# Warm-up products in bf16 in place of fp32, and first touches of the inputs moved close together

## The chip, the cores and the metric

The kernel runs on one core of a Trainium2 chip. The metric is the device time of one execution in microseconds. A core has a matrix engine (TensorE, PE in the profile; its weight loads are listed as PEld), a vector engine (DVE), a scalar engine (ACT), GpSimd (POOL) and a queue processor (SP). DMAs are issued by SP and, for a few, by ACT. The engines run side by side and wait for each other by semaphores.

## The reference

Linear attention over eight batches is followed by a feed-forward layer with exact GELU:

```python
q_s = exp(q - max(q, -1));  q_s = q_s / sum(q_s, -1)       # (8, 8, 576, 64), over the head dimension
k_s = exp(k - max(k, 2));   k_s = k_s / sum(k_s, 2)        # over the sequence
kv  = einsum('bhsd,bhse->bhde', k_s, v)
x   = einsum('bhsd,bhde->bhse', q_s, kv)                   # reshaped to (4608, 512)
h   = x @ w_in                                             # (512, 2048)
out = (0.5 * h * (1 + erf(h / sqrt(2)))) @ w_out           # (2048, 512)
```

The inputs are float32 and so is the output.

## The kernel before

The work is cut by batch. Of each batch the first 512 of the 576 sequence rows make one block of 512 tokens; the remaining 64 rows of all eight batches make a ninth block. A block goes through these steps, all products in bf16: `exp_q` and `exp_k` on ACT, `norm_q` (row sums, reciprocals and the product with them, on DVE and POOL), a transpose of the normalised q, `cast_v` (v to bf16 with a column of ones), `kv_mm` and `kv_norm` (k times v and the division by the column of sums), `x_mm` (q times kv), then `h_phase` (16 groups of four products with w_in into PSUM, each followed by a GELU on ACT) and `y_phase` (four groups of 16 products with w_out, copied by DVE and stored).

The order on each engine is the order in which the code issues the instructions (`manual_schedule`). The steps of the next batches are issued inside the loops of the current one, as functions that `h_phase` and `y_phase` call at given places.

Batch 0 has nothing before it to hide behind, and it is where the change lies. The order there is: ACT issues four small DMAs into the tile `touch` (line 423), SP issues the loads of q, k, v of batch 0, then w_in in five pieces (`load_wi`, line 363), three pieces of w_out, q and k of batch 1, and so on. DVE clears `zeros32` and `zeros` (lines 436 and 437). PE then multiplies zeros by zeros (`warm`, line 405), transposes the first half of q (line 212), multiplies zeros twice more, transposes the second half, multiplies zeros twice more, and goes on to `kv_mm` (line 166), four products of zeros in `warm_x` (line 413), `x_mm` (line 251) and the first `h_phase` (line 295). POOL normalises the first half of q (line 198), casts three quarters of v (line 145) and then the first two pieces of w_in (line 375); DVE casts the other pieces (line 379).

DMAs issued by SP and ACT share eight completion semaphores, given out in turn, so that a ninth DMA is not issued before the first has landed, and so on. The four touches take four of them.

Of the kernel before, what the change touches and what calls it, by code (L numbers as in the profile page):

```python
# [8 lines left out]
FP32 = mybir.dt.float32  # L9
# [7 lines left out]
def kernel(  # L17
# [16 lines left out]
    nc = tc.nc  # L34
# [9 lines left out]
    NS = S // 64  # L44
    VW = D + 2

    singles = ctx.enter_context(tc.tile_pool(name="singles", bufs=1))
# [19 lines left out]

    kvc = [singles.tile([128, HP, D], BF16, name=f"kvc{b}") for b in range(B)]
    zeros = singles.tile([128, 512], BF16)
    zeros32 = singles.tile([128, 512], FP32)  # L70
    scr = singles.tile([128, 2], FP32)

    def setup_tiles():
        nc.vector.memset(scr, 0.0)
        for i in range(2):
            nc.vector.memset(v_aug[i][:, :, :, D:D + 1], 1.0)
# [23 lines left out]
    def load(b):  # L100
        load_main(b, "q", q)
        load_pair(b, "k", k)
        load_pair(b, "v", v)
# [295 lines left out]
            out=wo_bf[:, 4 * i + c0:4 * i + c0 + n, :], in_=w[:, c0:c0 + n]  # L399
        )  # L400

    def warm(n, z=zeros):
        ps = psum_y.tile([128, DM], FP32, tag="y")
        for i in range(n):
            nc.tensor.matmul(ps, z[:, 0:128], z, start=True, stop=True)  # L405

    def warm_x():

# [6 lines left out]
                )  # L415

    touch = singles.tile([16, 4, 2], FP32)
    for i, a in enumerate((k[0].rearrange("h (p n) d -> (h p) (n d)", n=NS)[0:128:8, 0:2],  # L420
                           v[0].rearrange("h (p n) d -> (h p) (n d)", n=NS)[0:128:8, 0:2],
                           moe_w_in[0:128:8, 0:2], moe_w_out[0:512:32, 0:2])):
        nc.scalar.dma_start(out=touch[:, i, :], in_=a)


# [7 lines left out]
    wo.append(load_wo(3, 2))  # L433
    load_pair(1, "v", v, 4)
    load(2)
    nc.vector.memset(zeros32, 0.0)  # L436
    nc.vector.memset(zeros, 0.0)
    setup_tiles()
    warm(5, zeros32)


    table(AF.Exp)
# [5 lines left out]
    tp_evac(0, 0, "s")  # L448
    table(AF.Gelu)
    warm(2)  # L450
    cast_v(0, 0)
    for hp in range(1, HP):
        cast_v(0, hp, nc.gpsimd)
    cast_wi(0, wi[0], "p")
    cast_wi(1, wi[1], "p")
    tp_mm(0, 1)
    warm(2)
    for hp, pool, tag in ((0, psum_y, "y"), (1, psum_y, "y"), (2, psum_a, "a"), (3, psum_h, "h")):
        x_tile(0, hp, pool, tag)
# [151 lines left out]
```

## Time and profile before

| | us |
|---|---|
| median of 4 executions | 283.81 (283.62 to 283.97) |
| the profiled execution | 283.77 |
| its span, first to last instruction | 282.0 |
| PE busy | 269.8 |
| ACT busy | 156.8 |
| DVE busy | 102.1 |
| POOL busy | 32.9 |
| products of zeros at line 405, 14 records, sum | 8.1 |
| start of the first w_in product (line 295) | 14.76 |

A record in the timeline gives its start, its length, the engine, the line, the tiles with their sizes, a count, and in brackets how long the engine sat idle before it and what released it. PE records overlap, since products are pipelined: a product of 512 columns is recorded as 379 ns long while such products follow each other every 217 ns. A line of a table of stretches gives the stretch, its length, the busy time and count of each engine, the granted clock, the busy share of the DMA engines and their rate in GB/s.

### The profile page before, as it was taken

The numbers are of one execution on the slowest core, as the hardware profiler recorded it, in microseconds if no ns is written. First come the engines' busy times: TensorE is split into PE (matmuls) and PEld (weight loads), VectorE is DVE, ScalarE is ACT, GpSimd is POOL, SyncE is SP. The second block draws the span as 40 slices with busy tenths as digits, with TensorE's granted clock in tenths as the row PEclk, the third lists the DMA queues.
The fourth block names the chain that finished last, engine by engine and source line by source line (L and its number), as shares of the span: only waits on it lengthen the run. The fifth ranks groups of instructions, "written<-read, shape, count | busy, mean of one in ns | idle before, by whom it ended". The sixth has DMA issues, their size and how long they took to land.

```text
span 282.0 us, 4527 instructions
## 1 busy us (share of the span) xinstructions
PE 269.8 (96%) x1894; PEld 125.8 (45%) x1922; DVE 102.1 (36%) x150; ACT 156.8 (56%) x242; POOL 32.9 (12%) x25
## 2 busy tenths in 40 slices
PE   7799999999999899999999999999999999999993
PEld 3344454444444344444444444444444444444442
DVE  3766576309750560084007500651016100220011
ACT  5766654689377815692469346843683363136300
POOL 0530050002020050005000500050005000000000
PEclk9999999999999999999999999999999999999999
DMA  7999999953349339801991199117401500120033
GB/s 244 390 400 428 400 400 406 402 210 85 107 111 364 121 115 256 341 37 45 240 372 55 40 215 380 45 70 187 113 0 74 149 2 0 74 77 0 0 77 76
DMA packets 44852, 50.10 MB, mean 178 GB/s; under 512 B 20384, under 2 KB 29856, under 8 KB 44576
## 3 DMA queue, kind: packets, MB, share of 16 engines
q1 hardware_dynamic: 44544, 49.68, 51.6%
q8 instruction: 15, 0.25, 0.3%
q10 hardware_dynamic: 288, 0.13, 0.2%
q14 instruction: 5, 0.04, 0.0%
HBM read 36.70 MB, written 9.44 MB: 164 GB/s over the span
## 4 chain that ended last, share of the span: by engine, by line
PE 66%; DMA 23%; DVE 3%; ACT 3%; SPq 1%; issue 1%; ACTq 0%
PE ps L305 33%; PE ps L295 29%; DMA f<-in_v_dram 8%; DMA w<-in_moe_w_in_dram 6%; DMA f<-in_k_dram 5%; DMA out_dram<-y_sb 3%; DMA touch<-in_moe_w_out_dram 2%; PE kv L166 1%; PE ps L327 1%; DVE v_aug L145 1%; PE ps L251 1%; ACT ek L138 1%; DVE qsum L196 1%; ACT e L133 1%; DVE e L198 1%
## 5 line engine op out<-in xcount | busy, mean ns | idle before, releaser
L295 PE MATMUL ps<-xT,wi_bf 128*128 128x512 bf16 x565 | 125.4, 379 | 0.6
L305 PE MATMUL ps<-wo_bf,g 128*128 128x512 bf16 x543 | 122.3, 379 | 2.8 <-DVE y_sb L312 1.2
L300 ACT ACTIVATE g<-ps 128x512 bf16<-128x512 f32 x144 | 85.6, 597 | 67.3 <-PE ps L295 67.3
L295 PEld LDWEIGHTS <-wi_bf 128*128 128x128 bf16 x576 | 56.0, 98 | 68.4 <-issue 0.5
L305 PEld LDWEIGHTS <-g 128*128 128x128 bf16 x560 | 54.0, 98 | 65.6 <-issue 1.9
L312 DVE COPY y_sb<-ps 128x512 f32<-128x512 f32 x35 | 23.8, 683 | 75.2 <-PE ps L305 72.1
L198 POOL TENSOR_TENSOR e<-e,recq 128x2048 bf16<-128x2048 bf16 (+1 forms) x9 | 25.7, 2857 | 178.0 <-DVE recq L197 145.9
L145 DVE CAST v_aug<-f 128x576 bf16<-128x576 f32 x26 | 17.9, 745 | 57.3 <-DMA f<-in_v_dram 57.3
L277 ACT CAST xT<-ps 128x512 bf16<-128x512 f32 x19 | 10.2, 588 | 31.8 <-PE ps L251 22.2
L196 DVE TENSOR_REDUCE qsum<-e 128x16 f32<-128x1024 bf16 (+1 forms) x13 | 21.0, 1616 | 14.5 <-ACT e L133 14.5
L133 ACT ACTIVATE e<-f 128x512 bf16<-128x512 f32 (+1 forms) x42 | 20.5, 556 | 2.2 <-DMA f<-in_q_dram 2.0
L138 ACT ACTIVATE ek<-f 128x2304 bf16<-128x2304 f32 (+1 forms) x10 | 17.2, 1730 | 1.9 <-DMA f<-in_k_dram 1.8
L275 DVE CAST xT<-ps 128x512 bf16<-128x512 f32 x15 | 9.7, 686 | 15.4 <-PE ps L251 12.6
L79 ACT ACT_TABLE_LOAD x9 | 11.5, 1283 | 2.8 <-issue 2.6
L405 PE MATMUL ps<-zeros 128*128 128x512 f32 (+1 forms) x14 | 8.1, 722 | 1.5 <-DVE zeros L436 1.5
L133 ACT ACT_TABLE_LOAD x7 | 9.0, 1283 | 0.1
L166 PEld LDWEIGHTS <-ek 64*64 64x64 bf16 x576 | 6.6, 105 | 3.3 <-issue 1.6
L379 DVE CAST wi_bf<-w 128x512 bf16<-128x512 f32 (+1 forms) x8 | 7.1, 916 | 2.0 <-DMA w<-in_moe_w_in_dram 1.8
L166 PE MATMUL kv<-v_aug,ek 64*64 64x65 bf16 x576 | 7.4, 193 | 0.4 <-POOL v_aug L145 0.2
L398 DVE CAST wo_bf<-w 128x2048 bf16<-128x2048 f32 (+1 forms) x5 | 5.1, 1014 | 4.8 <-DMA w<-in_moe_w_out_dram 4.8
L198 DVE TENSOR_TENSOR e<-e,recq 128x1024 bf16<-128x1024 bf16 x4 | 6.4, 1600 | 0.1
L251 PE MATMUL ps<-qT,kvc 64*64 64x512 bf16 x60 | 5.0, 390 | 1.4 <-DVE kvc L177 1.4
(33 smaller groups left out, 41.5 us busy)
## 6 DMA issues: line engine op xcount, KB each, us to landing
out_dram<-y_sb SPq DMA_DIRECT2D x32, 256.0 KB, 2.3
f<-in_k_dram SPq DMA_DIRECT2D x6, 1152.0 KB, 9.7
f<-in_v_dram SPq DMA_DIRECT2D x6, 1152.0 KB, 11.5
f<-in_q_dram SPq DMA_DIRECT2D x6, 1024.0 KB, 7.3
w<-in_moe_w_in_dram SPq DMA_DIRECT2D x6, 512.0 KB, 8.1
f<-in_k_dram SPq DMA_DIRECT2D x4, 576.0 KB, 10.1
f<-in_v_dram SPq DMA_DIRECT2D x8, 288.0 KB, 8.2
f<-in_q_dram SPq DMA_DIRECT2D x4, 512.0 KB, 8.5
```

The lines of the kernel that those rows point to most:

```text
L79: nc.scalar.activation(out=scr[:, 1:2], in_=scr[:, 0:1], func=func)
L133: nc.scalar.activation(out=dst[:, i], in_=src[:, u], func=AF.Exp)
L138: nc.scalar.activation(out=ek[b % 2][:, i:i + n], in_=st[b]["kf"][:, i:i + n].rearrange("p x (n d) -> p x n d", n=NS), func=AF.Exp,)
L145: eng.tensor_copy(out=v_aug[b % 2][:, hp, :, 0:D], in_=st[b]["vf"][:, hp, :].rearrange("p (n d) -> p n d", n=NS),)
L166: nc.tensor.matmul(ps[c, i, half, 0:D + 1], ek[b % 2][pr, hp, n, :], v_aug[b % 2][pr, hp, n, 0:D + 1], start=(n == 0), stop=(n == NS - 1),)
L196: nc.vector.reduce_sum(out=qsum, in_=eq[:, :, hs, :], axis=AX.X)
L198: eng.tensor_tensor(out=eq[:, :, hs, :], in0=eq[:, :, hs, :], in1=recq.unsqueeze(3).to_broadcast([128, J, w, D]), op=ALU.mult,)
L277: nc.scalar.copy(out=st[b]["xT"][:, hp, :], in_=ps)
L295: nc.tensor.matmul(ps, wi_bf[:, dm, t * 128:(t + 1) * 128], xT[:, dm, :], start=(dm == 0), stop=(dm == NDM - 1),)
L300: nc.scalar.activation(out=g[:, t, :], in_=ps, func=AF.Gelu)
L305: nc.tensor.matmul(ps, st[c]["g"][:, t, j * 128:(j + 1) * 128], wo_bf[:, t, :], start=(t == 0), stop=(t == NDF - 1),)
L312: nc.vector.tensor_copy(out=y_sb, in_=ps)
```

## The change

The warm-up ahead of the first transposes is 25 products of bf16 zeros in place of five of fp32 zeros; the fp32 tile and its memset are gone. The four touches still read 16 times 8 bytes each, but from other rows. Of k and v they read the first 16 sequence rows of the first head, which lie in 4 KB, in place of 16 rows of 2304 bytes spread over the first 128 such rows. Of w_in they read rows 0 to 15 in place of every eighth of the first 128 rows; of w_out rows 0 to 15 in place of every 32nd of the first 512.

The order of every other instruction on every engine, and the waits of SP, ACT and POOL, are the same.

```diff
-    zeros32 = singles.tile([128, 512], FP32)
...
-    def warm(n, z=zeros):
+    def warm(n):
         ps = psum_y.tile([128, DM], FP32, tag="y")
         for i in range(n):
-            nc.tensor.matmul(ps, z[:, 0:128], z, start=True, stop=True)
+            nc.tensor.matmul(ps, zeros[:, 0:128], zeros, start=True, stop=True)
...
     touch = singles.tile([16, 4, 2], FP32)
-    for i, a in enumerate((k[0].rearrange("h (p n) d -> (h p) (n d)", n=NS)[0:128:8, 0:2],
-                           v[0].rearrange("h (p n) d -> (h p) (n d)", n=NS)[0:128:8, 0:2],
-                           moe_w_in[0:128:8, 0:2], moe_w_out[0:512:32, 0:2])):
+    for i, a in enumerate((k[0, 0, 0:16, 0:2], v[0, 0, 0:16, 0:2],
+                           moe_w_in[0:16, 0:2], moe_w_out[0:16, 0:2])):
         nc.scalar.dma_start(out=touch[:, i, :], in_=a)
...
-    nc.vector.memset(zeros32, 0.0)
     nc.vector.memset(zeros, 0.0)
     setup_tiles()
-    warm(5, zeros32)
+    warm(25)
```

## The prediction

> **What bounds the kernel now.** I read the page's busy times first, then what TensorE (PE) waits for, then the first 23 us in order of time, and last the DMA rate in short stretches.
>
> ```profile
> PE 269.8 (96%) x1894; PEld 125.8 (45%) x1922; DVE 102.1 (36%) x150; ACT 156.8 (56%) x242; POOL 32.9 (12%) x25
> ```
>
> PE is busy for 269.8 of 282.0 us. Whatever waits it has are few, and they are listed:
>
> ```profile
> PE ps L405 <- DVE zeros L436: 1.5, 1, 1.5
> PE ps L251 <- DVE kvc L177: 1.4, 3, 0.6
> PE ps L305 <- DVE y_sb L312: 1.2, 1, 1.2
> PE ps L212 <- POOL e L198: 1.0, 1, 1.0
> PE kv L166 <- POOL v_aug L145: 0.2, 1, 0.2
> ```
>
> Four of the five lie wholly or mostly before 14.8 us, where batch 0 is prepared; the exception is the 1.2 us at 98 us. From 14.76 us (the first product with w_in) on, PE does not wait before the kv step at 41.7 us for more than a few hundredths. So the end is set by **when that first product starts**, and by the pace of the loads while PE is just in time with them. What leads up to it:
>
> ```profile
> 9.33 0.62 PE L212 MATMUL ps<-identity,e 128*128 128x128 bf16 x8 [0.97 <-POOL e L198]
> 11.14 2.15 POOL L145 CAST v_aug<-f 128x576 bf16<-128x576 f32 x3 [1.87 <-DMA f<-in_v_dram]
> 11.86 0.47 PE L166 MATMUL kv<-v_aug,ek 64*64 64x65 bf16 x34 [0.17 <-POOL v_aug L145]
> 13.96 2.58 POOL L375 CAST wi_bf<-w 128x512 bf16<-128x512 f32 x4 [0.67 <-DMA w<-in_moe_w_in_dram]
> 14.41 0.41 PE L251 MATMUL ps<-qT,kvc 64*64 64x512 bf16 x4 [0.59 <-DVE kvc L177]
> 14.75 7.02 PEld L295 LDWEIGHTS <-wi_bf 128*128 128x128 bf16 x34 [0.23 <-POOL wi_bf L375]
> 22.14 6.16 PEld L295 LDWEIGHTS <-wi_bf 128*128 128x128 bf16 x30 [0.37 <-DVE wi_bf L379]
> ```
>
> (Start, length, engine, line, tiles, count, and in brackets the idle time and its releaser.) The v casts start when a load of v lands, the kv step waits for them, the w_in cast starts when w_in lands at 13.96, and at 22.14 the weights for w_in's fourth piece come just in time from its cast. All of it is the same load stream: q, k, v, w_in in this order. A stream later by d moves PE's whole remainder by about d. The warm-up product, by contrast, is over before 9.33, when PE waits for POOL's normalised q.
>
> The stream's rate (stretch, busy times, DMA share, GB/s at the end):
>
> ```profile
> 2.00:2.50 0.50, 0.50 (x2) 0.03 (x1) 0.01 (x1) 0.00 (x0) 0.00 (x0) 1.00 0.59 115
> 2.50:3.00 0.50, 0.50 (x2) 0.31 (x1) 0.00 (x0) 0.38 (x1) 0.00 (x0) 1.00 0.91 311
> 5.00:6.50 1.50, 1.50 (x4) 0.69 (x3) 0.79 (x1) 1.36 (x5) 0.00 (x0) 1.00 1.02 348
> 6.50:8.00 1.50, 1.50 (x5) 0.55 (x3) 1.47 (x3) 0.56 (x2) 0.63 (x1) 1.00 1.02 386
> 11.00:12.50 1.50, 1.33 (x44) 0.54 (x41) 0.28 (x2) 1.48 (x2) 1.30 (x2) 1.00 1.06 387
> ```
>
> Summing rate times length, 0.99 MB have moved by 5.0 us, 2.09 by 8.0 and 3.26 by 11.0. q is 1.05 MB, k and v 1.18 each: k begins at about 5.2 us, v at 8.4, w_in at 11.4. The stream runs near 390 GB/s once started.
>
> **The change part by part.** The sum is made against the profiled execution: 283.77 us, of which 282.0 are span and 1.8 lie around it. The median is 283.81, so the same number serves.
>
> *The fp32 memset goes.* It is 0.48 us of DVE, 0.91 to 1.39. The bf16 memset (0.27 us) takes its place and ends at 1.18; PE started 0.06 after its memset, so it starts at 1.24 in place of 1.45. DVE is next wanted at 5.71, after 3.70 us idle, and ACT's table load at 2.62 follows its own DMA issues. Gain on the path: 0.
>
> *Five fp32 products become 25 bf16 ones.* The weight loads tell the pace of the fp32 ones, and when the clock opens:
>
> ```profile
> 5.03 0.34 PEld L405 LDWEIGHTS ps<-zeros 128*128 128x128 f32 x1 [0.52 <-issue]
> 5.88 0.34 PEld L405 LDWEIGHTS ps<-zeros 128*128 128x128 f32 x1 [0.52 <-issue]
> 6.48 0.19 PEld L405 LDWEIGHTS ps<-zeros 128*128 128x128 f32 x1 [0.26 <-issue]
> 6.91 0.19 PEld L405 LDWEIGHTS ps<-zeros 128*128 128x128 f32 x1 [0.24 <-issue]
> ```
>
> Ten records: 0.85 us apart up to 5.88, then 0.43, so the speed doubles near 6.0, some 4.6 us after PE's start. A bf16 product of 512 columns takes 0.217 us warm (13.87 us for 64 of them after 14.76), half a warm fp32 record; slow, I take half of 0.85, 0.427. If the doubling again comes 4.6 us after the start, at 5.84, then 4.60 / 0.427 = 10.8 products are slow, 14.2 x 0.217 = 3.1 us follow, and the warm-up ends at 8.9. Before it ends at 8.36. The transposes cannot start before 9.27, when POOL ends its product: the 0.5 us later is hidden, with 0.4 to spare. Past that, PE sits 0.4 us idle before the kv step at 11.47, so about 0.75 us in all before lateness shows, one for one. The 45 more PE instructions stand ahead of the transposes only. Cost taken 0, by the row that shows the opening. Bounds: 0, and 2.25 if it never opened before the transposes (25 x 0.427 = 10.7 us, so the end is at 11.9, less the cover up to 9.67).
>
> A rule to weigh: the Trainium skill, "TensorE: Matmul & The Clock Gate", Part 1, says that the gate opens after a busy window of about 3.4 us which runs free of the program. An estimate by that rule alone puts the opening 3.4 to 6.8 us after the start, the end of the 25 between 8.3 and 10.0, and the cost between 0 and 0.35 us, where the row gives 0. The rule speaks against this change, since 25 products outlast the 20 half-records of before in every phase of such a window.
>
> *The rest of PE's order* (two warm products behind each transpose group, four between kv and x) is the same in both, so the gap of 0.97 us before 9.33 only shrinks. 0.
>
> *The four touches move.* ACT still issues four DMAs of 16 times 8 bytes (0.44 us each). k and v are now read within 4 KB, w_in within 16 rows and w_out within 16 rows, where they were spread over 8 times or more of that. Two costs can follow.
>
> First, landing:
>
> ```profile
> touch<-in_k_dram ACTq DMA_DIRECT2D x1, 0.1 KB, 2.2
> touch<-in_moe_w_out_dram ACTq DMA_DIRECT2D x1, 0.1 KB, 5.3
> ```
>
> SP's issues wait for touches, since eight completion semaphores are shared in turn: the first part of w_in is issued at 7.46, just as the w_out touch lands. SP waits 1.1 us there. But at 7.46 3.41 MB were issued and only 1.89 moved: 1.5 MB, or 3.9 us, still stand ahead of it. Sooner landing gains nothing, up to some 2 us later costs nothing. 0.
>
> Second, the first bytes of each tensor. q is touched by nothing, and its start is slow: until 3.0 only 0.23 MB moved against 1.5 us x 390 = 0.59, a loss of 0.9 us, part of which must be plain start-up. k, touched, shows 348 in place of 390 for 1.5 us: a loss of 0.16. v and w_in show none. If the rows near a touch are what saves this, moving them away brings a loss back for k, v and w_in. Against it: the rows of w_in from 128 on, and most of k and v, are touched in neither kernel and stream at 386 to 393. Bounds: 0.16 gained (k's dip goes, nothing comes), and 2.6 lost (three tensors at 0.9, less k's 0.16). I take the row nearest, k's dip, for v and w_in as well: 2 x 0.16 = 0.3.
>
> Sum: 0 + 0 + 0 + 0.3 = **0.3 us, 284.1**, which is within 0.2% (0.57 us, about what a measurement of this kernel can tell from no change).
>
> **The rivals.**
> *A, the touches matter more* (slower): k, v and w_in each start as slowly as half of q's start, 3 x 0.45 less 0.16 = 1.2, so 285.0. For it: q's slow start, and that the old touches lay at every eighth of the first 128 rows that the loads read, the new ones at one end. Against: no dip at untouched rows. It decides, that is passes 0.57, once each start loses 0.25.
> *B, the warm-up runs long* (slower): the clock opens late and the 25 push the transposes, the kv step and the first w_in product, by up to the 2.25 worked above, half of it as the middle case: 284.9. It decides when more than 0.75 + 0.57 us are added to the end at 8.9, which takes six more slow products, an opening 2.7 us later than the trace's. Against: at the trace's pace 14 of the 25 come after the opening.
> *C, faster*: touches that fall close together return sooner and leave the engines to q in its start, while they land now at 2.2 to 5.3 us beside it. If half of the 0.9 us comes back and k's dip goes, 0.45 + 0.16 = 0.6 is gained, 283.2, since q, k, v and w_in all move up. It decides at two thirds of q's loss. Against: 64 reads of 8 bytes are nothing beside 1 MB.
> *D, nothing at all*: only hidden things move, 283.8.
>
> **How the numbers follow.** Forecast with D (283.5 to 284.4): 0.41. A: 0.31. B: 0.09. C: 0.19. So faster 0.19, same 0.41, slower 0.40. The range reaches from C with a little more (283.0) to past A (285.3, that is 1.5 lost); the upper bounds of A and B are left out. The forecast's own range is 283.3 to 284.4.
>
> **What would show it.** Right: 25 warm-up products ending near 8.9, transposes still released by POOL's product near 9.3, w_in's first cast near 14.0 to 14.3 and the first w_in product as much later; the rate at 8 to 9.5 and 11 to 12.5 us dipping by some 10%. A: rates under 300 there, and the w_in cast after 14.9. B: bf16 products still 0.43 apart after 8 us, the transposes after 9.6. C: the stream past 300 GB/s before 2.5 us. I am wrong if PE waits later than 14.8 us change by more than the start did.

## The result, and the profile after

The changed kernel takes 283.10 us (median of 39 executions, 282.44 to 283.64) where the kernel before takes 283.81 (59 executions): a ratio of 0.9974, 95% interval 0.9968 to 0.9981, so 0.7 us faster. The forecast was 0.3 us slower. The profiled execution of the changed kernel took 283.21 us with a span of 281.4, against 283.77 and 282.0.

The front of the kernel, on which the prediction was spent, went nearly as it said. The timeline of the changed kernel (line numbers are lower by one from the tiles on, by three at the touches and by four behind the memset of the zeros):

```profile
1.19 7.90 PE L404 MATMUL ps<-zeros 128*128 128x512 bf16 x25 [1.19 <-DVE scr L73]
5.43 0.15 PEld L404 LDWEIGHTS <-zeros 128*128 128x128 bf16 x1 [0.28 <-issue]
5.86 2.73 PEld L404 LDWEIGHTS <-zeros 128*128 128x128 bf16 x13 [0.27 <-issue]
9.40 0.62 PE L211 MATMUL ps<-identity,e 128*128 128x128 bf16 x8 [0.32 <-POOL e L197]
13.92 2.56 POOL L374 CAST wi_bf<-w 128x512 bf16<-128x512 f32 x4 [0.63 <-DMA w<-in_moe_w_in_dram]
14.75 3.78 PEld L294 LDWEIGHTS <-wi_bf 128*128 128x128 bf16 x19 [0.23 <-POOL wi_bf L374]
19.70 9.39 PEld L294 LDWEIGHTS <-wi_bf 128*128 128x128 bf16 x45 [1.17 <-DVE wi_bf L378]
```

The 25 products run from 1.19 to 9.09, their weight loads 0.43 us apart up to 5.86 and half that after it. The transposes still wait for POOL. The first w_in product starts at 14.76 in both kernels. The one difference is a wait of 0.68 us on PE for w_in's third piece, at 19.70; most of it is made good at the kv step of batch 1, where the kernel before waited 0.4 us.

In the profiled executions, one of each kernel, PE's last product ends at 277.55 us before and at 277.66 after: 0.1 us **later**. Yet the span is 0.5 us shorter. So everything that this pair gains, and 0.1 more, lies behind PE's last product, in the last 4 us, which the prediction did not look at. The DMA issues of the kernel before in the last 5 us (tiles, queue, count, size, us from issue to landing), and what SP waits for there (us in total, times, the longest):

```profile
out_dram<-y_sb SPq DMA_DIRECT2D x1, 96.0 KB, 2.2
out_dram<-y_sb ACTq DMA_DIRECT2D x1, 96.0 KB, 2.8
out_dram<-y_sb SPq DMA_DIRECT2D x1, 32.0 KB, 2.9
out_dram<-y_sb ACTq DMA_DIRECT2D x1, 32.0 KB, 3.1
```

```profile
SPq L606 <- DMA out_dram<-y_sb: 2.5, 2, 1.7
```

The same of the changed kernel:

```profile
out_dram<-y_sb SPq DMA_DIRECT2D x1, 32.0 KB, 2.0
out_dram<-y_sb ACTq DMA_DIRECT2D x1, 32.0 KB, 2.1
```

```profile
SPq L602 <- DMA out_dram<-y_sb: 1.6, 2, 1.3
```

The last two stores, the same in both programs, land 0.9 and 1.0 us sooner. What else the DMA engines carried then stands in the DMA queues between 279 and 281 us (packets, MB, share of the time of 16 DMA engines). Of the kernel before:

```profile
q10 hardware_dynamic: 135, 0.09, 17.3%
q1 hardware_dynamic: 82, 0.03, 6.1%
q14 instruction: 1, 0.01, 1.0%
```

Of the changed kernel:

```profile
q10 hardware_dynamic: 157, 0.13, 21.4%
q1 hardware_dynamic: 96, 0.04, 7.1%
```

In the kernel before, one packet of queue 14, an instruction fetch, stands among the last stores; in the changed kernel it does not. The packet records behind these views tell more:

```
kernel before   instruction packet, 8192 bytes, starts 279.47, 0.31 us
                last five store packets of 512 bytes: 279.85 to 280.19, 68 to 85 ns each (from 279.42 to 279.82: 25 to 40)
                last store: 15 of its 16 parts landed by 280.12, the last part at 281.00
changed kernel  instruction packet, 8192 bytes, starts 281.74, after the last instruction
                no store packet of 512 bytes over 60 ns after 279.4
                last store: 15 of 16 parts landed by 280.15, the last part at 280.18
```

A store is done when its last part is. Of each of the last two stores one part of 16 came 0.9 us after the other fifteen (the other store's at 280.82, its fifteenth at 279.91). The records do not name the DMA engine; the reading is that one engine fetched instructions while its parts of the last stores stood in its queue. How a fetch of 0.31 us makes 0.9 is not shown: the late packets end 0.6 us after the others, and 0.3 us more than for the others passes from there to the landing.

Whose instructions? The change takes one instruction from DVE, a memset, and adds 45 to PE by the prediction's count (the trace has 30 records more, half of them weight loads). In the trace, DVE's own steps point to itself: two of its steps in the barrier at the program's end, where the engines wait for each other, 0.12 us apart in the kernel before, are 0.48 apart in the changed one (280.62 and 281.10), and the same gap appears 128 recorded instructions earlier, at 68.19. 8192 bytes are 128 instructions of 64 bytes, if 64 is taken as the size. An earlier fetch of queue 14 also moves, from 65.83 to 69.38 us; the other three of the span stay near 40, 106 and 170. So the theory to test, **T**: DVE's last instruction fetch falls where DVE's instruction count puts it; one instruction fewer moves it from among the last stores to behind them. The rivals are **F1**, the touches, and **F2**, the bf16 warm-up. All three can be separated by kernels that change one and keep the rest. A further rival is the place in memory: without the fp32 tile, by the code, every tile behind it lies 2048 bytes lower in each partition.

### The profile page after: what moved, and what is told of

Read it like the earlier page. It is cut to its first block, busy times and chain, and to the rows that moved or that the text cites. A ratio compares the mean times of both kernels' runs of the same rounds, so it can differ in the third digit from the quotient of the medians.

```text
span 281.4 us, 4556 instructions
## 1 busy us (share of the span) xinstructions
PE 270.7 (96%) x1909; PEld 126.0 (45%) x1937; DVE 101.8 (36%) x149; ACT 156.8 (56%) x242; POOL 32.9 (12%) x25
## 4 chain that ended last, share of the span: by engine, by line
PE 81%; DMA 10%; DVE 3%; ACT 2%; issue 1%; SPq 1%; ACTq 0%
PE ps L304 38%; PE ps L294 38%; DMA f<-in_v_dram 6%; DMA w<-in_moe_w_in_dram 3%; PE kv L165 2%; DMA f<-in_q_dram 1%; PE ps L250 1%; PE ps L326 1%; DVE v_aug L144 1%; DVE qsum L195 1%; ACT ek L137 1%; ACT e L132 1%; DVE e L197 1%; SPq L230 0%; DVE y_sb L311 0%
## 5 line engine op out<-in xcount | busy, mean ns | idle before, releaser
L404 PE MATMUL ps<-zeros 128*128 128x512 bf16 x29 | 9.1, 476 | 1.2 <-DVE scr L73 1.2
```

## The experiments

Times are medians; ratios are to the kernel before on the same chip, with 95% intervals. "Tail" is the span's end less the end of PE's last product, in the profiled execution. What was found in all of them:

| run | DVE instructions against before | last fetch, us after PE's end | tail, us | time, us | ratio |
|---|---|---|---|---|---|
| kernel before | 0 | 1.9 | 4.41 | 283.81 | |
| changed kernel | -1 | 4.1 | 3.77 | 283.10 | 0.9974 (0.9968 to 0.9981) |
| touch_only | 0 | 1.9 | 4.42 | 283.75 | 0.9997 (0.9979 to 1.0016) |
| warm_bf16_same_count | 0 | 1.9 | 4.53 | 283.94 | 1.0000 (0.9988 to 1.0011) |
| fp32_one_memset | -1 | 4.1 | 3.76 | 282.81 | 0.9957 (0.9940 to 0.9974) |
| after_one_more | 0, and a new tile | 2.0 | 4.45 | 287.37 | 1.0110 (1.0075 to 1.0145) |
| after_scr_twice | 0 | 1.9 | 4.43 | 283.97 | 0.9997 (0.9985 to 1.0009) |
| after_pad8 | -1, and a new tile | 4.1 | 3.77 | 286.65 | 1.0102 (1.0077 to 1.0127) |
| after_five_more | +4 | -2.3 | 3.44 | 282.55 | 0.9957 (0.9942 to 0.9971) |
| after_three_fewer | -4 | 4.6 | 3.45 | 283.04 | 0.9972 (0.9952 to 0.9992) |
| before_four_more | +4 | -2.2 | 3.44 | 282.57 | 0.9953 (0.9933 to 0.9973) |
| before_four_more_touch | +4 | -2.0 | 3.46 | 282.99 | 0.9974 (0.9959 to 0.9988) |
| after_five_more_again | +4 | -2.3 | 3.46 | 282.97 | 0.9972 (0.9957 to 0.9986) |

**The touches alone**, in the kernel before:

```diff
-    ... k[0].rearrange("h (p n) d -> (h p) (n d)", n=NS)[0:128:8, 0:2], ...
+    ... k[0, 0, 0:16, 0:2], v[0, 0, 0:16, 0:2], moe_w_in[0:16, 0:2], moe_w_out[0:16, 0:2] ...
```

> The kernel before with the four new touches and nothing else. Theory T (the gain is in the tail: one DVE instruction fewer moves DVE's last 8 KB instruction fetch from 279.5 us, amid the last stores, to after them): DVE's instructions are those of before, so the fetch stays and the time is that of before, 283.8 within 0.2, with the last store landing some 3 us after its issue. Rival F1 (the touches give the gain): 283.1.

No gain: 0.9997, and a tail of 4.4 us. F1 falls.

**The warm-up alone**, with the now unread fp32 tile still cleared:

```diff
-    warm(5, zeros32)
+    warm(25)
```

> The kernel before with the 25 bf16 warm-up products, but the fp32 memset kept, so that DVE has as many instructions as before. Theory T: 283.8 within 0.2, and the fetch among the last stores. Rival F2 (the warm-up in bf16 gives the gain, by 45 more PE instructions or by a warmer clock): 283.1.

1.0000, tail 4.5. F2 falls: neither the 45 PE instructions nor the other clock history in the first 9 us is worth anything.

**One DVE instruction fewer**, with the old warm-up and touches:

```diff
-    zeros = singles.tile([128, 512], BF16)
     zeros32 = singles.tile([128, 512], FP32)
+    zeros = zeros32[:, 0:256].bitcast(BF16)
...
-    nc.vector.memset(zeros, 0.0)
```

> The kernel before, fp32 warm-up and old touches kept, with one DVE instruction fewer: the bf16 zeros are the first half of the cleared fp32 tile, and their own memset goes. Theory T: 283.1 within 0.2, the last DVE fetch after the last stores, which land 2.0 to 2.4 us after their issue. Rivals F1 and F2: 283.8.

The whole gain is there, 0.9957 (the interval overlaps with the changed kernel's), and the fetch and tail are those of the changed kernel. In this kernel the warm-up and the touches, which the change was about, are the old ones. Its SP wait and landings at the end:

```profile
SPq L605 <- DMA out_dram<-y_sb: 1.5, 2, 1.3
```

```profile
out_dram<-y_sb SPq DMA_DIRECT2D x1, 32.0 KB, 2.0
out_dram<-y_sb ACTq DMA_DIRECT2D x1, 32.0 KB, 2.1
```

**One DVE instruction more in the changed kernel**, first with a tile of its own:

```diff
     zeros = singles.tile([128, 512], BF16)
+    extra = singles.tile([128, 2], FP32)
...
     nc.vector.memset(zeros, 0.0)
+    nc.vector.memset(extra, 0.0)
```

> The changed kernel with one more DVE instruction, a memset of 8 bytes a partition behind that of the zeros, where DVE is idle. Theory T: the fetch is back among the last stores and the time back at 283.8 within 0.2. Rivals F1 and F2: 283.1, since touches and warm-up are those of the changed kernel.

The tail went back to 4.4 us, as T says, but the time went to 287.37: 3.5 us too much, and all of it ahead of PE's end, which came at 281.78. This run changed two things at once, an instruction and an address: the new tile moves every tile behind it by 8 bytes. Two runs take these apart, one with the instruction and no tile, one with the tile and no instruction:

```diff
         nc.vector.memset(scr, 0.0)
+        nc.vector.memset(scr, 0.0)
```

> The changed kernel with the 8-byte memset of the tile scr issued twice: as many DVE instructions as the kernel before, and no tile more, so that no address moves. Theory T (the place of DVE's last instruction fetch): 283.8, the span's end 4.4 us after PE's end as in the kernel before. Rival A (the 4 us that the run with a new 8-byte tile lost come from the instruction itself): 287.

```diff
+    pad = singles.tile([128, 2], FP32)
     scr = singles.tile([128, 2], FP32)
```

> The changed kernel with an unused tile of 8 bytes a partition ahead of scr and no instruction more. Theory B (the run with the new tile lost its other 3.5 us because every later tile, the targets of the loads among them, moved by 8 bytes): 286.6, the loads' rate between 30 and 50 us near 380 GB/s in place of 402, and the end still 3.8 us after PE's end. Rival A: 283.1.

The instruction gives 0.9997 and a tail of 4.4: the changed kernel with its gain undone by one memset of 8 bytes that DVE issues in an idle time at 1 us. That is T's clearest run, and since all tiles lie there as in the changed kernel, the place in memory falls as a rival too. Its landings and SP's wait at the end are again those of the kernel before:

```profile
out_dram<-y_sb SPq DMA_DIRECT2D x1, 32.0 KB, 2.9
out_dram<-y_sb ACTq DMA_DIRECT2D x1, 32.0 KB, 3.1
SPq L603 <- DMA out_dram<-y_sb: 2.5, 2, 1.7
```

The tile gives 286.65 with a tail of 3.8, as theory B has it: the moved addresses cost the time, and not the instruction. The loads' rate is the last number of each stretch; of the changed kernel:

```profile
15.00:30.00 15.00, 14.22 (x65) 6.34 (x66) 10.05 (x11) 9.70 (x17) 1.38 (x3) 1.00 1.04 411
30.00:50.00 20.00, 19.82 (x174) 9.39 (x175) 13.16 (x21) 11.35 (x19) 3.90 (x4) 1.00 1.05 402
```

Of the run with the unused 8 bytes:

```profile
15.00:30.00 15.00, 14.73 (x64) 6.46 (x63) 9.28 (x11) 8.92 (x16) 1.90 (x4) 0.89 1.04 401
30.00:50.00 20.00, 19.16 (x170) 9.13 (x172) 13.95 (x21) 10.48 (x17) 3.90 (x4) 1.00 1.06 380
```

The DMA engines are as busy and carry 2.4 and 5.5% less. In the packet records, the mean packet of 2304 bytes up to 60 us takes 99.4 ns in place of 94.9, one of 1024 bytes 50.1 in place of 46.9, while DVE's copies of y take 683 ns in place of 684. The loads are slower; DVE is not. The Trainium skill, "DMA: Bandwidth & Descriptors", section on how a descriptor splits into AXI transactions, describes extra beats for a descriptor that starts off a 256-byte boundary, and speaks of bytes that are fetched; here the source in DRAM did not move, only the target in SBUF, and no run here shows the beats. So why the packets take 3 to 5 ns more is open. In the pad run the granted clock also falls to a half from 15.0 to 18.4 us (the 0.89 above), and in the run with the tile `extra` from 101.9 to 105.4; in no other profile here does it fall before PE's end. That is the smaller part of the loss: of the pad run's six executions two had a mean granted clock of 1.000 and still took 286.35 and 285.59 us, 2.5 to 3.3 more than the changed kernel; the four at 0.993 and 0.994 took 286.33 to 287.90, on average 1.1 more than those two.

**Moving the fetch further away**, to earlier and to later:

```diff
-        nc.vector.memset(scr, 0.0)
+        for i in range(6):
+            nc.vector.memset(scr, 0.0)
```

> The changed kernel with the memset of scr issued six times: four DVE instructions more than the kernel before. Theory T: the last fetch is asked for some four instructions earlier, behind the copy at 274 us, and is over before the last stores are issued; DVE has no stall at its last barrier either (0.48 us between its last two barrier steps in the changed kernel, 0.12 before). The end 3.4 us after PE's, 282.7. Rival C (any number of DVE instructions above the changed kernel's loses): 283.8.

```diff
-        nc.vector.memset(scr, 0.0)
+        nc.gpsimd.memset(scr, 0.0)
         for i in range(2):
-            nc.vector.memset(v_aug[i][:, :, :, D:D + 1], 1.0)
+            nc.gpsimd.memset(v_aug[i][:, :, :, D:D + 1], 1.0)
```

> The changed kernel with three of its DVE memsets (scr and the two of v_aug) issued on POOL, which is idle there. Theory T: DVE's stream ends at or ahead of the place that asks for the last fetch, so there is no fetch and no stall: the end 3.4 us after PE's, 282.7. Rival C': fewer instructions bring nothing beyond the first one, 283.1.

Both have the tail of 3.4 us that was expected, 0.3 less than the changed kernel, and DVE's stall at the last barrier is gone too (0.11 us between the two steps). With five memsets more, the fetch starts at 275.64, ahead of the last stores. With three fewer it still takes place, at 281.97, after the last instruction; that there would be none was wrong. The times, 282.55 and 283.04, have intervals that overlap with each other's and with that of the changed kernel, so the last 0.3 us is shown in the profiles and not in the times; by its time alone, 283.04, rival C' would fit as well.

**Are touches or warm-up worth anything besides?** With the fetch out of the way in all three, on one chip. The first two are the kernel before, without and with the new touches, and with this edit; the third is the changed kernel with five memsets more, again:

```diff
-        nc.vector.memset(scr, 0.0)
+        for i in range(5):
+            nc.vector.memset(scr, 0.0)
```

> The kernel before, fp32 warm-up and old touches, with the memset of scr issued five times, so that DVE's instruction count is that of the fastest kernel so far (the changed one with five memsets more). Theory T: the end 3.4 us after PE's, about 1.0 us less than the kernel before, 282.8. Rivals F1 and F2 (touches or warm-up are worth something besides): 283.1 or more, since both are those of the kernel before.

> The same with the new touches as well: fp32 warm-up, DVE's count as in the run beside it. Theory T: the same time as that run, within 0.2. The prediction's term (the first rows of v and w_in stream 0.3 us later under the new touches): 0.3 more.

> The changed kernel with the memset of scr issued six times, again, on the chip of the two runs beside it: bf16 warm-up and new touches, the same DVE count. Theory T: the same time as those two within 0.2, with PE's end alike and 3.4 us behind it.

The kernel before, with four memsets added, is at 282.57: its ratio is below the changed kernel's (0.9953 against 0.9974), but the intervals overlap. The two runs with the new touches are 0.4 us above it, where T expected 0.2 at most. The means of 7 and 12 executions (282.59 and 282.96, standard deviation 0.45) differ by 0.37 with an interval of about 0.45 to either side, and the run touch_only showed nothing of the kind. So a cost of the new touches of some tenths is neither shown nor excluded. The bf16 warm-up costs nothing that can be seen: 282.99 and 282.97.

## Why the prediction was wrong

*The step that failed* is the first term of the sum, put at nothing: "The fp32 memset goes ... Gain on the path: 0." DVE is idle where the memset stood, and as work it costs nothing; that was right. But it is also an instruction, and DVE's instruction count sets where in time its last fetch falls. Taking it away brought the last store's landing from 3.45 us after PE's end (281.00 less 277.55) to 2.52 (280.18 less 277.66), a gain of 0.93; of that the new stall at the last barrier gave back 0.3, by the time from the landing to the end of the span (281.95 less 281.00 is 0.95, 281.43 less 280.18 is 1.25). The tail became 0.63 shorter, where the medians differ by 0.71.

*The frame that let it happen*: the prediction said that the end is set by when the first w_in product starts, and costed only what lies ahead of it. The profile of before had the lines against that. Its last two stores of 32 KB landed 2.9 and 3.1 us after their issue, while the larger ones of 96 KB just ahead took 2.2 and 2.8, and the page counts five instruction packets in queue 14:

```profile
q14 instruction: 5, 0.04, 0.0%
```

No rival covered the tail. The faster one, C, named 283.2, which is near the measured 283.10, but by luck: its gain was to lie in the start of the stream, which was to pass 300 GB/s before 2.5 us. From 2.0 to 2.5 us it ran at 150 GB/s (115 before), and PE's first w_in product starts at 14.76 in both. C's threshold was off as well: with k's dip counted, as in its 0.6, a gain of 0.57 needs under half of q's 0.9 and not two thirds.

*The warm-up term* was right in its cost of 0: 25 products ending at 9.09 where 8.9 was predicted, an opening of the clock near 5.9, where 5.84 was, and transposes released by POOL with 0.32 us to spare; the run with it alone is at 1.0000. That the opening came so near the predicted place was in part luck: over all thirteen profiles the granted clock opens between 2.8 and 5.9 us after PE's first product, not at a fixed 4.6. The rule on a window that runs free, which the prediction weighed, has such a spread, 3.4 to 6.8 in its estimate; the 2.8 of fp32_one_memset lies below that, and there the measurement decides. In the eight kernels with the bf16 warm-up the products of zeros end between 8.42 and 9.29 us, ahead of the transposes in each; rival B did not occur. The cover itself was over-read: the 0.4 us of idle time at 11.47 stand in the row of the weight loads, PE's row there has none, and in the changed kernel the transposes and the kv step start 0.07 us later alike (9.40 and 11.54). And the list of PE's waits lacked a row, 1.1 us in seven pieces put down to issue; nothing hangs on it.

*The 45 PE instructions* were put ahead of the transposes only, at no cost; that held.

*The touches' landing* was right: 1.8, 3.4, 4.3 and 5.3 us, and w_in's first part issued at 7.44.

*The touches' 0.3 us*, the whole of the forecast, was not seen where it was put. v and w_in begin without a dip:

```profile
5.00:6.50 1.50, 1.50 (x6) 0.64 (x5) 0.72 (x1) 1.36 (x5) 0.00 (x0) 1.00 1.01 323
8.00:9.50 1.50, 1.18 (x8) 0.40 (x6) 1.43 (x3) 1.16 (x1) 1.34 (x1) 1.00 1.04 395
11.00:12.50 1.50, 1.45 (x46) 0.62 (x43) 0.28 (x2) 1.48 (x2) 1.33 (x2) 1.00 1.06 388
```

395 and 388 GB/s stand where 389 and 387 stood, and only k's dip is deeper, 323 in place of 348, which is 0.1 us of stream. Nor does the first w_in product come later: with the new touches it starts between 14.57 and 14.76 us in seven profiles (without those of a new tile), with the old ones between 14.63 and 15.08 in four. Rival A, with 1.2 us, falls. The prediction's own sign of being wrong, later waits of PE that change by more than that start did, came true with the 0.68 us at 19.7, but this is not where the gain came from. The wait for w_in's third piece at 19.7 us is not a matter of the touches: before_four_more, with the old ones, has it too.

```profile
PE ps L296 <- DVE wi_bf L380: 0.9, 1, 0.9
```

## What to carry to other kernels

An instruction that costs no time where it stands can still cost or save time at the far end, as DVE's memset did here, because it shifts where its engine's later instruction fetches fall; in a program whose last stores and fetches share DMA engines, read the landing times of the last stores and the instruction queue's packets first, and compare the end of the last product with the end of the span. Before a change of a few tenths of a per cent is credited to what it was about, put the instruction counts back (a repeated tiny memset does) and measure again. Such a dummy must not bring a new tile with it, or the addresses behind it move.

## What was not expected of the hardware

An instruction fetch of 8 KB, 0.31 us long, among the last stores goes with a final part of the last store that lands 0.85 to 0.99 us after the fifteenth, in five profiles; in the eight others here it lands 0.03 us after it at most. The Trainium skill, "Runtime: NRT & Kernel Launch", section on instruction fetch mechanics, calls the cost of crossing a block mostly hidden and gives the block as 16 KiB. The runs here show packets of 16384 bytes on queue 8 but of 8192 on queue 14, and the crossing was not hidden at the end: the tail is 4.4 us or more wherever the fetch meets the last stores, against 3.4 where it falls elsewhere, and 3.8 where DVE stalls for 0.36 us between its barrier steps. What DVE waits for there is open: the fetch's own packet starts 0.64 us after that stall has ended (281.74 against 281.10).

Eight bytes of unused SBUF ahead of the load targets cost 3.5 us, more than one per cent, with slower loads (402 to 380 GB/s) and, in part of the executions, a lower clock, as told above.

A part of the spread between executions, 282.4 to 283.6 in the changed kernel, may come from where PE's end falls: in the eleven profiled kernels without a new tile it lies between 277.06 and 278.17 us. What sets that was not looked into.
